# Strided sparse attention and a Mish MLP: strided v of every batch cast in flight, local q and k of batch 3 issued earlier, MLP1 opening with two strided halves

## The chip, the cores and the metric

The kernel runs on one core of a Trainium2 chip. The time is device microseconds of one execution; three runs of the kernel before gave 307.52, 309.35 and 312.32, median 309.35. The profile is of one further execution, in which every instruction and every DMA packet was recorded.

## The reference

There are 8 batches of 8 heads, 576 positions, head size 64, all in f32. Scores are `q k^T / 8`; heads 0 to 3 see the last 32 positions (local), heads 4 to 7 see positions congruent modulo 32 (strided). Softmax, times v. The result, seen as 4608 tokens of width 512, goes through an MLP with an activation:

```python
mask_local = (rel >= 0) & (rel < stride)                        # stride = 32
mask_strided = (rel >= 0) & (pos[None, :] % stride == pos[:, None] % stride)
attn = softmax(where(mask, scores, -1e9));  x = attn @ v        # 4608 x 512
h = x @ w_in                                                    # 512 x 2048
g = h * np.tanh(np.log1p(np.exp(h)))                            # Mish
out = g @ w_out                                                 # 2048 x 512
```

## The kernel before

**Blocks and batches.** The MLP works on nine blocks of 512 tokens, the attention on eight batches of 576. Both are interleaved on TensorE in an order written out by hand: block t consists of MLP1 (x times `w_in`, Mish on ScalarE into `gT`) and MLP2 (`gT` times `w_out`), and the attention of batch t+1 is threaded between the steps of MLP2 of block t, by the list `at`: at[i] runs after step i. Attention leaves its result transposed in `xT`, a ring of four batches: chunks 2 and 3 of `xT` are the strided heads, chunks 0 and 1 the local ones. Each product in `mlp1` adds the strided chunks (2, 3) first and the local ones (0, 1) after; group g covers two slices of 128 hidden columns in one accumulator of two PSUM banks, `accs[g % 3]` for g not of the form 3n+2, and single banks otherwise. For blocks 1 to 8 group 0 is split in its strided half and its local half, which run one after the other; the other seven groups follow whole.

MLP2 of block 0 is a plain product; its 16 steps end with two stores of 512 KB. MLP2 of blocks 1 to 7 uses seven products instead of eight (`mlp2_seven`): VectorE forms sums of `gT` and of `w_out`, and the results are copied and added up in two output tiles `osb`. The tiles come from a pool of three buffers. The first copy that ScalarE makes in block t is c22, into the second `osb` of the block; c11, VectorE's, goes into the first.

**Where q, k and v come from.** A batch's strided q and k are loaded on GpSimd's DMA queue, which converts f32 to bf16 on the way (`load_qk_str`, L119). Local q and k and local v are loaded as f32 on SP's queue (`load_qk_loc`, L133; `load_v_loc`, L169) and then cast by GpSimd (`cast_qk_loc`, `cast_v_loc`, L191). There is one f32 buffer for each: `kl32`, `ql32`, `vl32`. Strided v has two ways: for batches 0 to 2 it is loaded in bf16 on GpSimd's queue (`load_early_v_str`, L152) into one half of the buffer `vs32`, and spread from there into `vs` (`spread_v_str`); for batches 3 to 7 it is loaded as f32 on SP's queue (`load_v_str`, L143), into all of `vs32`, and cast by GpSimd (`cast_v`). Then SP transposes strided and local k and q of a batch by DMA (`transpose_by_dma`, L209 and L215), six instructions per batch from batch 2 on.

**The order on SP's queue.** SP issues in program order, and its instruction ends when its transfer has been passed on; the transfers of one queue run behind one another. In block 0, `load_rest2` runs after step 12 of MLP2: the six transposes of batch 2, then local v of batch 2. Then come block 0's two stores (after steps 13 and 15, L595), then, at the end of the block, local k and q, strided v and local v of batch 3. In a later block t: the transposes of batch t+2 (after step 10), the two stores of the block (L554), then the four loads of batch t+3.

**The order on GpSimd.** In block 0: casts of local v of batch 1 and of local k and q of batch 2; strided k and q of batch 3 (DMA); casts of local v of batch 2, which wait for its load. In block t from 1 to 4: strided k and q of batch t+3 (DMA, at the end of MLP1); the masks of the local scores of batch t+1 (L330); after step 9 of MLP2 the casts of batch t+2: local k, local q, strided v, local v.

In blocks 3 to 6 the last of the local attention (`late`) runs in the MLP1 of the next block, after its first, second and sixth entries.

Of the kernel before, what the change touches and what calls it, by code (L numbers as in the profile page):

```python
# [10 lines left out]
F32 = mybir.dt.float32  # L11
BF16 = mybir.dt.bfloat16
# [8 lines left out]
CS, PN = 8, 72  # L21
# [22 lines left out]
def kernel(ctx, tc, q, k, v, moe_w_in, moe_w_out, out):  # L44
    nc = tc.nc
    B, H, S, D = q.shape
# [9 lines left out]
    const = ctx.enter_context(tc.tile_pool(name="const", bufs=1))  # L56
# [8 lines left out]
    stm_bias = consts[0:PN, 128 + 2 * WQ + PN:128 + 2 * WQ + 2 * PN]  # L65
    zeros = const.tile([128, 512], BF16, name="zeros")
    vl32 = const.tile([128, 4, NW, D], F32, name="vl32")
    vs32 = const.tile([128, 4, CS, D], F32, name="vs32")
    ql32 = const.tile([128, 4, CL, D], F32, name="ql32")
    kl32 = const.tile([128, 4, CL, D], F32, name="kl32")  # L70
    ql = [const.tile([128, CL, 4, D], BF16, name=f"ql{i}") for i in range(2)]
# [4 lines left out]
    vs = [const.tile([128, 4, CS, D + 1], BF16, name=f"vs{i}") for i in range(2)]  # L76
# [23 lines left out]
    def acc(i, name):  # L100

        pool = ps_z[0] if i == 2 else ps_a
        return pool.tile([128, 2, 512], F32, tag=f"acc{i}", name=name)

    def bank(i, name):

        return ps_z[0].tile([128, 512], F32, tag=f"bank{i}", name=name)

    def split_third():

        third.close()
        ps_z[0] = third.enter_context(tc.tile_pool(name="psy", bufs=1, space=PS))
# [5 lines left out]
    def load_str(b, dst, src, h0=0):  # L118
        nc.gpsimd.dma_start(  # L119
            dst[b % 2][0:PN, h0:4, :], src[b, 4 + h0:8].rearrange("h (p j) d -> p h (j d)", j=CS)  # L120
        )

    def load_qk_str(b):
        load_str(b, ks, k)
        load_str(b, qs, q)
# [5 lines left out]
    def load_qk_loc(b):  # L131
        for dst, src in ((kl32, k), (ql32, q)):
            nc.sync.dma_start(  # L133
                dst[0:PL].rearrange("p h i d -> p (h i) d"),
                src[b, 0:4].rearrange("h (i p) d -> p (h i) d", p=PL),
            )
# [2 lines left out]
        for dst, src in ((kl, k), (ql, q)):  # L139
            nc.gpsimd.dma_start(by_head(dst[b]), src[b, 0:4].rearrange("h (p j) d -> p h (j d)", j=CL))  # L140

    def load_v_str(b):
        nc.sync.dma_start(vs32[0:PN], v[b, 4:8].rearrange("h (p j) d -> p h j d", j=CS))  # L143

    def vs_raw(b):

        flat = vs32[:].rearrange("p h j d -> p (h j d)").bitcast(BF16)
        b = b % 2
        return flat[0:PN, 2048 * b:2048 * b + 2048].rearrange("p (h x) -> p h x", h=4)

    def load_early_v_str(b):
        nc.gpsimd.dma_start(vs_raw(b), v[b, 4:8].rearrange("h (p j) d -> p h (j d)", j=CS))  # L152

    def spread_v_str(b, eng):
        cast(eng, vs[b % 2][0:PN, :, :, 0:D], vs_raw(b).rearrange("p h (j d) -> p h j d", d=D))

    def load_v_loc(b):

        w0 = 0
        if b == 0:
            w0 = 1
            nc.sync.dma_start(vl32[32:128, 0, 0, :], v[0, 0, 0:96, :])
        first = v[b, 0:1, 0:1, :].offset + (w0 * WQ - 32) * D
        src = bass.AP(v.tensor, first, [[D, 128], [WQ * D, 4 * NW - w0], [1, D]])
        nc.sync.dma_start(vl32[:].rearrange("p h w d -> p (h w) d")[:, w0:, :], src)  # L169

    def load_v(b):
        load_v_str(b)
        load_v_loc(b)

    def load_w_in(f0, f1):
        nc.gpsimd.dma_start(
# [10 lines left out]
    def cast(eng, out_, in_):  # L187
        if eng is nc.scalar:
            nc.scalar.copy(out_, in_)  # L189
        else:  # L190
            eng.tensor_copy(out_, in_)  # L191
# [15 lines left out]
    def transpose_by_dma(b):  # L207
# [5 lines left out]
        for hp in range(2):  # L213
            for src, dst in ((kl, kTl[:, hp, 32:32 + S]), (ql, qTl[:, hp, :])):
# [1 line left out]
                    dst.rearrange("c (i n) -> c i n", i=NW),  # L216
                    by_tile(src[b % 2])[:, hp].rearrange("p i e d -> p (i e d)"),
                )

    def cast_v(b, e_s, e_l):  # L220
        cast(e_s, vs[b % 2][0:PN, :, :, 0:D], vs32[0:PN])
        cast_v_loc(b, e_l)

    def cast_v_loc(b, eng, i0=0, i1=NW):
        for i in range(i0, i1, 3):
            cast(
                eng, vl[b % 2][:, i:i + 3, :, 0:D],
                vl32[:, :, i:i + 3, :].rearrange("p h w d -> p w h d"),
            )
        if i0 == 0:  # L230
            eng.memset(vl[b % 2][0:32, 0, :, 0:D], 0.0)
# [234 lines left out]
    def mlp1(t, accs):  # L466
        gT = g_pool.tile([128, 16, 512], BF16, tag="gT", name="gT")
        Sg = g_pool.tile([128, 4, 8, 256], BF16, tag="Sg", name="Sg") if t > 0 else None

        held, tiles = {}, {}  # L470

        def group(g, ccs=(2, 3, 0, 1)):
            single = t > 0 and g % 3 == 2
            if g not in held:
                if single:
                    held[g] = [bank(u, "psb") for u in range(2)]
                else:
                    ps = acc(accs[g % 3], "psh")
                    held[g] = [ps[:, u, :] for u in range(2)]
                    tiles[g] = ps  # L480
            for u in range(2):
                ps_u = held[g][u]
                fc = g + 8 * u if t > 0 else 2 * g + u
                for a, n, o in segs(t):
                    for cc in ccs:
                        nc.tensor.matmul(  # L486
                            ps_u[:, o:o + n], lhsT=w_in[:, cc, fc * 128:(fc + 1) * 128],
                            rhs=xT[:, cc, a:a + n], start=(cc == 2 and (o == 0 or len(ccs) == 4)),
                            stop=(cc == 1), skip_group_check=(len(ccs) < 4),
                        )  # L490
                if ccs[-1] == 1 and single:
                    nc.scalar.activation(gT[:, g + 8 * u, :], ps_u[:], AF.Mish)  # L492
            if ccs[-1] == 1:
                if not single:
                    to = gT[:, g::8, :] if t > 0 else gT[:, 2 * g:2 * g + 2, :]
                    nc.scalar.activation(to, tiles[g][:], AF.Mish)  # L496
                if t < B - 1 and g == 7:
                    nc.scalar.preload_act_table(AF.Exp)
                if t > 0 and g in SUMS_AT:
                    sums_g(gT, Sg, *SUMS_AT[g])  # L500
        if t == 0:
            halves = [[lambda g=g, c=c: group(g, c) for g in range(3)] for c in ((2, 3), (0, 1))]
            return gT, halves[0], halves[1] + [lambda g=g: group(g) for g in range(3, 8)]
        return gT, Sg, [lambda: (group(0, (2, 3)), group(0, (0, 1)))] + [
            lambda g=g: group(g) for g in range(1, 8)
        ]

    SUMS_AT = {3: (0, 4), 5: (4, 6), 6: (6, 7), 7: (7, 8)}

# [153 lines left out]
    with tc.manual_schedule():  # L663
        Po, Dv, Sc = nc.gpsimd, nc.vector, nc.scalar
# [6 lines left out]
        first = v[0, 0:1, 0:1, :].offset + 64 * D  # L671
# [21 lines left out]
        for h in (2, 3):  # L693
            first = v[0, h:h + 1, 0:1, :].offset - 32 * D
# [51 lines left out]
        gT, g1s, g1 = mlp1(0, accs)  # L746
# [22 lines left out]
        def load_rest2():  # L769
            transpose_by_dma(2)  # L770
            load_v_loc(2)
            load_qk_str(3)
            cast_v_loc(2, Po)

        for t in range(NBLK):
            if t == 0:
                x, y, z = accs
                (at, ts), late = attn_steps(1, y, y), {}
                at[0].append(cast_v1)
                at[12].append(load_rest2)  # L780
                at[15].append(lambda: spread_v_str(2, Dv))
                out_accs = (z, x)
            else:
                if t == 1:
                    split_third()
                x, y = 0, 1
                gT, Sg, g1 = mlp1(t, (x, y))
                now = late
                at, late = attn_steps(t + 1, x, y) if t + 1 < B else ([], {})
                if t + 2 < B:  # L790
                    at[10].append(lambda: transpose_by_dma(t + 2))
            for i, g in enumerate(g1):
                g()
                if t == 0:
                    for s in ts if i == len(g1) - 1 else ():
                        s()
                    continue
                if t == 1 and i == 0:
                    sums_w()
                for s in now.get(i, ()):  # L800
                    s()
            if 0 < t < B - 3:
                load_qk_str(t + 3)
            if t == 0:
                steps = mlp2(t, gT, out_accs, fc_major=True)
            elif t == NBLK - 1:
                mlp2_last(t, gT, Sg)
                break
            else:
                za, zc = [bank(i, "pso")[:].rearrange("p (n o) -> p n o", n=2) for i in range(2)]  # L810
                steps = mlp2_seven(t, gT, Sg, za, zc)
            for i, g in enumerate(steps):
                g()
                if i < len(at):
                    for s in at[i]:
                        s()
                if t > 0 and i == 9 and t + 2 < B:
                    cast_qk_loc(t + 2, Po, Po)
                    cast_v(t + 2, Po, Po)
            if t + 3 < B:  # L820
                load_qk_loc(t + 3)
                load_v(t + 3)


# [28 lines left out]
```

## Time and profile before

| what | value |
|---|---|
| runs | 307.52, 309.35, 312.32 us (median 309.35) |
| the profiled execution: its own time, its span | 308.23 us, 306.5 us |
| TensorE busy | 294.7 us (96%), 2900 matmuls and transposes |
| ScalarE, VectorE, GpSimd busy | 172.2, 152.4, 103.8 us |
| SP's DMA queue (q1) | 88120 packets, 33.00 MB, 62.6% of 16 engines |
| GpSimd's DMA queue (q0) | 14800 packets, 11.04 MB, 25.2% of 16 engines |
| stores of `osb` in the chain that ended last | 6% of the span |
| granted TensorE clock | 1.00 |

The span runs from the first to the last instruction. A busy share of TensorE near 100% does not say that nothing waits: matmul ends are modelled and pipelined. A row of a timeline gives start, duration, engine, line, operation and tiles, and in brackets the idle time in front of it with what ended it. An engine name with a q (SPq) is the engine's queue of instructions, here its DMA issues. Tiles are written output<-input, with buffer numbers left out. The chain is the sequence of work followed back from the last instruction; its rows give start, length and what.

### The profile page before, as it was taken

How to read it: one execution, taken by the hardware profiler on the slowest of the kernel's cores; microseconds unless marked ns; L12 is line 12 of the kernel's file. 1: busy time of each engine (PE TensorE's matmuls, PEld its weight loads, DVE VectorE, ACT ScalarE, POOL GpSimd, SP SyncE). 2: the span in 40 equal slices, each digit the busy share in tenths (PEclk: the TensorE clock that was granted, in tenths of full speed). 3: DMA queues.
4: the chain of work that ended last, by engine and by line, in shares of the span. 5: the costliest groups of instructions: out<-in, count | busy, mean ns of one | idle time of the engine just before them, and what ended most of it. 6: DMA issues, size and time to landing. Idle time of an engine off the chain costs nothing.

```text
span 306.5 us, 6863 instructions
## 1 busy us (share of the span) xinstructions
PE 294.7 (96%) x2900; PEld 198.5 (65%) x2922; DVE 152.4 (50%) x356; ACT 172.2 (56%) x220; POOL 103.8 (34%) x111
## 2 busy tenths in 40 slices
PE   8989999899999989999999999999999999999995
PEld 3554556445884568547888886468646874685484
DVE  2270165867670856256634753475437553720642
ACT  1568634667555665657556854676467646514530
POOL 8284502460664408620690059004900320000000
PEclk9999999999999999999999999999999999999999
DMA  8999999979999999999999999799950021003003
GB/s 155 185 203 186 194 195 193 168 123 157 263 141 182 156 250 186 163 134 260 182 169 116 262 188 156 189 180 187 131 161 0 3 98 41 2 0 139 0 0 139
DMA packets 103238, 44.72 MB, mean 146 GB/s; under 512 B 85672, under 2 KB 97272, under 8 KB 103208
## 3 DMA queue, kind: packets, MB, share of 16 engines
q1 hardware_dynamic: 88120, 33.00, 62.6%
q0 software_dynamic: 14800, 11.04, 25.2%
q8 instruction: 23, 0.38, 0.6%
q10 hardware_dynamic: 288, 0.25, 0.3%
q14 instruction: 7, 0.06, 0.1%
HBM read 38.38 MB, written 9.44 MB: 156 GB/s over the span
## 4 chain that ended last, share of the span: by engine, by line
PE 81%; DMA 9%; ACT 5%; DVE 3%; issue 2%; POOL 0%; ACTq 0%; POOLq 0%
PE psh L486 29%; PE pso L559 24%; PE psb L486 8%; DMA out_dram<-osb 6%; PE pso L587 4%; PE pso L614 4%; PE po L346 4%; PE ps L316 3%; DMA qs<-in_q_dram 3%; DVE x_l L372 2%; ACT Ps L324 1%; PE trx L395 1%; PE trx L385 1%; DVE osb L538 1%; ACT Pl L324 1%
## 5 line engine op out<-in xcount | busy, mean ns | idle before, releaser
L486 PE MATMUL psh<-xT,w_in 128*128 128x512 bf16 (+1 forms) x484 | 101.1, 358 | 1.7 <-ACT xT L189 0.8
L486 PEld LDWEIGHTS <-w_in 128*128 128x128 bf16 x640 | 61.4, 98 | 59.6 <-issue 2.3
L496 ACT ACTIVATE gT<-psh 128x1024 bf16<-128x1024 f32 x56 | 57.0, 1024 | 45.5 <-PE psh L486 45.5
L330 POOL TENSOR_TENSOR Pl<-Pl,consts_sb 128x960 bf16<-128x960 bf16 (+1 forms) x18 | 29.2, 1634 | 82.9 <-ACT Pl L324 82.4
L511 DVE TENSOR_TENSOR Sg<-gT 128x256 bf16<-128x256 bf16 (+2 forms) x64 | 27.2, 427 | 55.6 <-ACT gT L496 53.6
L559 PEld LDWEIGHTS <-Sg 128*128 128x128 bf16 x448 | 41.9, 98 | 6.2
L559 PE MATMUL pso<-Tw,Sg 128*128 128x256 bf16 x336 | 40.1, 273 | 0.0
L559 PEld LDWEIGHTS <-gT 128*128 128x128 bf16 x336 | 31.4, 98 | 4.6
L189 ACT COPY xT<-trx 128x576 bf16<-128x576 bf16 x32 | 20.1, 640 | 19.9 <-PE trx L395 13.9
L189 ACT COPY osb<-pso 128x512 f32<-128x512 f32 (+1 forms) x26 | 14.2, 545 | 29.3 <-PE pso L559 14.5
L486 PE MATMUL psb<-xT,w_in 128*128 128x512 bf16 (+1 forms) x141 | 30.1, 355 | 0.2
L559 PE MATMUL pso<-w_out,gT 128*128 128x256 bf16 x224 | 27.8, 273 | 0.0
L324 ACT ACTIVATE Pl<-ps 128x960 bf16<-128x960 f32 (+1 forms) x24 | 19.2, 808 | 11.7 <-PE ps L316 11.4
L538 DVE TENSOR_TENSOR osb<-pso,osb 128x512 f32<-128x512 f32 x21 | 14.5, 692 | 21.7 <-PE pso L559 20.0
L191 POOL CAST vl<-vl 128x768 bf16<-128x768 f32 x15 | 12.8, 881 | 27.2 <-DMA vl<-in_v_dram 27.2
L324 ACT ACTIVATE Ps<-ps 72x864 bf16<-72x864 f32 (+1 forms) x24 | 18.5, 804 | 4.9 <-PE ps L316 4.8
L492 ACT ACTIVATE gT<-psb 128x512 bf16<-128x512 f32 x32 | 19.0, 596 | 3.5 <-PE psb L486 3.5
L372 DVE TENSOR_TENSOR x_s<-po,rden 72x512 bf16<-72x512 f32 x28 | 19.2, 686 | 1.0
L330 DVE TENSOR_TENSOR Ps<-Ps,consts_sb 72x864 bf16<-72x864 bf16 (+1 forms) x21 | 12.2, 580 | 9.4 <-ACT Ps L324 8.8
L587 PE MATMUL pso<-w_out,gT 128*128 128x512 bf16 x59 | 15.8, 380 | 0.5 <-issue 0.3
L346 PEld LDWEIGHTS <-Ps 72*128 72x128 bf16 x256 | 12.1, 97 | 5.4 <-DVE Ps L330 1.7
L357 DVE RECIPROCAL rden<-po 96x4 f32<-96x4 f32 (+1 forms) x22 | 3.9, 177 | 22.1 <-PE po L346 22.0
(90 smaller groups left out, 346.3 us busy)
## 6 DMA issues: line engine op xcount, KB each, us to landing
out_dram<-osb SPq DMA_DIRECT2D x16, 512.0 KB, 4.8
vl<-in_v_dram SPq DMA_DIRECT2D x7, 768.0 KB, 11.2
kl<-in_k_dram SPq DMA_DIRECT2D x6, 576.0 KB, 10.2
ql<-in_q_dram SPq DMA_DIRECT2D x6, 576.0 KB, 13.1
vs<-in_v_dram SPq DMA_DIRECT2D x5, 576.0 KB
qs<-in_q_dram POOLq DMA_DIRECT2D x8, 288.0 KB, 8.9
w_in<-in_moe_w_in_dram POOLq DMA_DIRECT2D x4, 512.0 KB, 10.2
w_out<-in_moe_w_out_dram POOLq DMA_DIRECT2D x4, 512.0 KB, 17.2
```

The costliest lines, as they stand in the source:

```text
L189: nc.scalar.copy(out_, in_)
L324: nc.scalar.activation(pt[0:n, :, 0:nw], ps[0:n, :, o0:o0 + nw], AF.Exp, scale=scale)
L330: meng.tensor_tensor(out=pm, in0=pm, in1=mk[0:n, :].unsqueeze(1).unsqueeze(1).to_broadcast([n, 2, nu, w]), op=ALU.mult,)
L346: nc.tensor.matmul(po[:, h, :], lhsT=pt[0:n, c0:c0 + 128], rhs=rhs, start=True, stop=True,)
L372: nc.vector.tensor_tensor(out=dst.rearrange("p e (h d) -> p e h d", h=4), in0=po[0:m, :, :, 0:D], in1=rden[0:m].unsqueeze(3).to_broadcast( ...
L486: nc.tensor.matmul(ps_u[:, o:o + n], lhsT=w_in[:, cc, fc * 128:(fc + 1) * 128], rhs=xT[:, cc, a:a + n], start=(cc == 2 and (o == 0 or len( ...
L492: nc.scalar.activation(gT[:, g + 8 * u, :], ps_u[:], AF.Mish)
L496: nc.scalar.activation(to, tiles[g][:], AF.Mish)
L511: nc.vector.tensor_tensor(out=out_, in0=in0, in1=in1, op=op)
L538: add = lambda o, p: nc.vector.tensor_tensor(out=o, in0=p, in1=o, op=ALU.add)
L559: nc.tensor.matmul(ps[:, pair, :], lhsT=lhs(c, 128 * pair), rhs=rhs(c), start=(first and pair == 0 and c == 0), stop=(last and c == 7), sk ...
L587: nc.tensor.matmul(p[:, ot % 2, :], lhsT=gT[:, fc, 128 * ot:128 * ot + 128], rhs=w_out[:, fc, :], start=(fc == 0), stop=(fc == 15),)
```

## The change

Three edits. (1) Strided v of batches 3 to 7 is loaded as batches 0 to 2 were, in bf16 on GpSimd's queue, right behind strided k and q of the batch; the buffer is now a bf16 tile with two halves, `vsr`, of the same size as `vs32`; GpSimd spreads it into `vs` where it cast it before. SP no longer carries it. (2) The loads of local k and q of batch 3 move on SP's queue from behind block 0's two stores to a place in front of them, at the end of `load_rest2`'s SP work. (3) In the MLP1 of blocks 1 to 8 the strided half of group 1 runs between the two halves of group 0, and group 1's local half is the second entry of the list; the list keeps its eight entries.

```diff
-    vs32 = const.tile([128, 4, CS, D], F32, name="vs32")
+    vsr = const.tile([128, 2, 4, CS * D], BF16, name="vsr")
...
     def vs_raw(b):
-        flat = vs32[:].rearrange("p h j d -> p (h j d)").bitcast(BF16)
-        b = b % 2
-        return flat[0:PN, 2048 * b:2048 * b + 2048].rearrange("p (h x) -> p h x", h=4)
+        return vsr[0:PN, b % 2]
...
-        return gT, Sg, [lambda: (group(0, (2, 3)), group(0, (0, 1)))] + [
-            lambda g=g: group(g) for g in range(1, 8)
-        ]
+        first = [lambda: [group(*x) for x in ((0, (2, 3)), (1, (2, 3)), (0, (0, 1)))], lambda: group(1, (0, 1))]
+        return gT, Sg, first + [lambda g=g: group(g) for g in range(2, 8)]
...
         def load_rest2():
             transpose_by_dma(2)
             load_v_loc(2)
+            load_qk_loc(3)
             load_qk_str(3)
+            load_early_v_str(3)
             cast_v_loc(2, Po)
...
             if 0 < t < B - 3:
                 load_qk_str(t + 3)
+                load_early_v_str(t + 3)
...
                     cast_qk_loc(t + 2, Po, Po)
-                    cast_v(t + 2, Po, Po)
+                    spread_v_str(t + 2, Po)
+                    cast_v_loc(t + 2, Po)
             if t + 3 < B:
-                load_qk_loc(t + 3)
-                load_v(t + 3)
+                if t > 0:
+                    load_qk_loc(t + 3)
+                load_v_loc(t + 3)
```

More of the change, by code (lines that the diff above doesn't have):

```diff
@@ L140, in load_early_loc @@
             nc.gpsimd.dma_start(by_head(dst[b]), src[b, 0:4].rearrange("h (p j) d -> p h (j d)", j=CL))
-    def load_v_str(b):
-        nc.sync.dma_start(vs32[0:PN], v[b, 4:8].rearrange("h (p j) d -> p h j d", j=CS))
     def vs_raw(b):
-        flat = vs32[:].rearrange("p h j d -> p (h j d)").bitcast(BF16)
-        b = b % 2
-        return flat[0:PN, 2048 * b:2048 * b + 2048].rearrange("p (h x) -> p h x", h=4)
+        return vsr[0:PN, b % 2]
     def load_early_v_str(b):
@@ L169, in load_v_loc @@
         nc.sync.dma_start(vl32[:].rearrange("p h w d -> p (h w) d")[:, w0:, :], src)
-    def load_v(b):
-        load_v_str(b)
-        load_v_loc(b)
     def load_w_in(f0, f1):
@@ L218, in transpose_by_dma @@
                 )
-    def cast_v(b, e_s, e_l):
-        cast(e_s, vs[b % 2][0:PN, :, :, 0:D], vs32[0:PN])
-        cast_v_loc(b, e_l)
     def cast_v_loc(b, eng, i0=0, i1=NW):
```

## The prediction

> **What bounds the kernel now.** I read the span by stages first (windows cut where TensorE passes from MLP1 to MLP2), then ScalarE's order of time, the chain, and the queues behind it. Columns of the windows: stretch, its length, busy us of TensorE, its weight loads, VectorE, ScalarE, GpSimd (with counts), granted clock, DMA share, GB/s.
>
> ```profile
> 73.81:91.64 17.83, 17.35 (x253) 15.14 (x252) 12.32 (x28) 11.15 (x15) 9.97 (x10) 1.00 1.25 202
> 105.71:124.77 19.06, 17.54 (x254) 15.18 (x253) 11.78 (x28) 11.15 (x15) 8.24 (x8) 1.00 1.22 212
> 138.84:155.99 17.15, 16.89 (x240) 14.48 (x239) 10.96 (x26) 11.31 (x14) 8.10 (x8) 1.00 1.24 218
> ```
>
> These are the MLP2 stages of blocks 1, 2 and 3. TensorE bounds the kernel (294.7 us busy of 306.5); block 3 shows the clean stage, 17.15 us. Block 1 loses 0.7 us and block 2 loses 1.9 us. What they wait for is in ScalarE's timeline (brackets: idle time before, and what ended it):
>
> ```profile
> 79.77 0.59 ACT L189 COPY osb<-pso 128x512 f32<-128x512 f32 x1 [1.75 <-DMA out_dram<-osb]
> 112.89 0.59 ACT L189 COPY osb<-pso 128x512 f32<-128x512 f32 x1 [2.98 <-DMA out_dram<-osb]
> ```
>
> and in the chain (start, length, what):
>
> ```profile
> 67.36 12.33 DMA out_dram<-osb
> ...
> 106.84 5.94 DMA out_dram<-osb
> ```
>
> The output tiles `osb` rotate through three buffers. Block 1's second tile is the third one taken after block 0's first, so its first ScalarE copy (c22) may start only when block 0's **first store** has landed, at 67.36 + 12.33 = 79.7. ScalarE runs in order and the next exponentials stand behind that copy; TensorE needs them for the local scores. So this landing has no slack at all: it holds ScalarE 1.75 us already. Block 2 hangs on block 1's first store in the same way.
>
> The store's data was ready at 57.2. It is late because of SP's queue (start, duration of the issue):
>
> ```profile
> 65.41 1.23 SPq L215 DMA_TRANSPOSE qTl<-ql  x1
> 66.69 0.58 SPq L169 DMA_DIRECT2D vl<-in_v_dram  x1
> 67.36 8.37 SPq L595 DMA_DIRECT2D out_dram<-osb  x2
> 75.78 0.88 SPq L133 DMA_DIRECT2D kl<-in_k_dram  x1
> 76.71 4.95 SPq L133 DMA_DIRECT2D ql<-in_q_dram  x1
> 81.77 8.34 SPq L143 DMA_DIRECT2D vs<-in_v_dram  x1
> 90.22 0.40 SPq L169 DMA_DIRECT2D vl<-in_v_dram  x1
> ```
>
> The reader sees an SP that is never idle here: an issue of 5 to 8 us is an issue held back by transfers not yet drained. Landings from the issue lists (issue plus time to landing) come in the order of issue: local v of batch 2 at 66.69 + 11.2 = 77.9, the stores at 79.7 and 81.8 (75.31 + 6.5), local k and q of batch 3 at 87.1 and 93.0.
>
> **The edit ahead of the stores.** The new `load_qk_loc(3)` in `load_rest2` puts these two loads, 576 KB each, between local v of batch 2 and block 0's first store on SP. Their buffers are free (GpSimd's casts of batch 2 end at 64.5), so nothing holds them but the queue. Their price, from the issue lists of 66 to 92 us, then of 108 to 126 us:
>
> ```profile
> kl<-in_k_dram SPq DMA_DIRECT2D x1, 576.0 KB, 11.3
> ql<-in_q_dram SPq DMA_DIRECT2D x1, 576.0 KB, 16.3
> ```
> ```profile
> kl<-in_k_dram SPq DMA_DIRECT2D x1, 576.0 KB, 9.7
> ql<-in_q_dram SPq DMA_DIRECT2D x1, 576.0 KB, 12.0
> ```
>
> In the second pair they follow a store landed at 114.2 and land at 117.7 and 120.9: 6.7 us for both, with no GpSimd load in flight. In the first pair they follow the store of 81.8 and take 11.2 us, beside two GpSimd loads (qs and ks of batch 4). So a GpSimd load beside them costs about (11.2 - 6.7)/2 = 2.2 us. The queues' lists for 74:76, where SP's queue is alone, and for 82:88, say the same (packets, MB, share of 16 engines):
>
> ```profile
> q1 hardware_dynamic: 1631, 0.42, 135.0%
> ```
> ```profile
> q0 software_dynamic: 772, 0.57, 83.4%
> q1 hardware_dynamic: 1230, 0.31, 52.6%
> ```
>
> SP's queue (q1) moves 815 packets a us alone and 205 beside GpSimd's (q0).
>
> Do GpSimd's loads of batch 4 fall into this stretch again? They stand behind the cast of batch 2's local v, which starts when that has landed:
>
> ```profile
> 77.93 1.97 POOL L191 CAST vl<-vl 128x768 bf16<-128x768 f32 x2 [12.04 <-DMA vl<-in_v_dram]
> ...
> 80.09 0.72 POOL L119 DMA_DIRECT2D ks<-in_k_dram  x1
> ```
>
> They do. And the change makes them three, since strided v of batch 4 follows on the same queue; strided v of batch 3 likewise follows ks and qs of batch 3 at 65.9, ahead of local v of batch 2. The sum for the first store's landing: 79.7, plus 2.0 for v of batch 3 (0.834 x 6 us x 288/772 packets = 1.9; a load beside costs 2.2), plus 6.7 for k and q, plus 5.0 for the batch-4 loads (three at 2.2 make 6.6; I let the last fall partly behind the store) = 93.4. Bounds: 86.4 if no GpSimd load counts; 97 if all count and SP's queue runs empty for 2 us, as between 90 and 92, when it moved 465 packets instead of 1630. I take 93.4, nearest to the row of 11.2 us, the same two loads in the same place. The c22 copy, and all behind it on ScalarE, TensorE, VectorE and GpSimd's masks, comes **13.7 us** later than now (bounds 6.7 and 17.3).
>
> **What is given back.** Batch 3's k and q are there before block 1's casts, and strided v's issue leaves SP: the transposes of batch 3 and then block 1's stores no longer wait, relative to TensorE, as they do up to 106.84. Block 2's 1.9 us go. Nothing is late next: blocks 3 to 6 have clean MLP2 stages (17.15 to 17.2) in front of an SP that was later than it will be now. -1.9 (0 if the delayed stretch repeats the pattern).
>
> **MLP1's order.** Four matmuls of group 1 (0.216 us each, 1.73 per 8) move ahead of group 0's local half, which waits for the last copy of xT:
>
> ```profile
> 60.87 2.75 PE L486 MATMUL psh<-xT,w_in 128*128 128x512 bf16 x12 [0.81 <-ACT xT L189]
> ```
>
> At block 1 the cover is worth up to 0.8 us, but the landing time ends block 1's next stage whatever TensorE did before: nothing. At blocks 2 and 3 the four matmuls end 0.25 us before the copy does (91.64 + 0.86 against 92.76): -0.5 for both, 0 to -0.75. Blocks 4 to 8 show no such wait: 0. The first Mish comes 0.86 us later; ScalarE idles 1.17 us ahead of it, and that accumulator is wanted again only by group 3, 5.2 us in: 0, or 0.9 at most once if the cover is gone.
>
> **Strided v on GpSimd.** Its 288 packets leave q1 and join q0, about 1.9 us of the engines' time either way. Each load costs GpSimd 0.70 us of issue (as L152 does for batches 0 to 2), queued behind it are masks before which GpSimd idles 10 to 19 us (1.3 in block 1): 0. The cast then reads bf16 instead of f32, 72x2048 on GpSimd: that form is not in the trace; its f32 twin takes 1.89, and anything between 0.7 (VectorE's copy of this form) and 3 disappears in the same idle time. The local transposes wait for the k and q casts ahead of it, not for it. 0.
>
> **TensorE's clock.** While ScalarE is held, TensorE stops at the local scores (now 0.44 us before 81.32), then for some 14 us. What a rest does shows only at the start:
>
> ```profile
> 1.20 6.43 PE L270 MATMUL un<-zeros 128*128 128x512 bf16 x16 [1.20 <-DVE zeros L678]
> ```
>
> 402 ns each against 216 later: 3.0 us lost on sixteen. Rests of under 1 us cost nothing. So 0 to +3.0; a rest of 14 us is nearer to the start, and as some matmuls behind it wait for exponentials anyway I take +2.0. The Trainium skill (TensorE: Matmul & The Clock Gate, Part 1: The HAM clock gate) says that about 3.4 us without work halve the clock and that about 3.4 us of work restore it, an estimated 1.7 us here instead of 2.0; the profile's granted clock, 1.00 throughout, begins its records too late to show the start, so no row decides.
>
> **Sum.** 13.7 - 1.9 - 0.5 + 2.0 = +13.3 on the profiled execution's 308.23 (span 306.5): 321.5. That execution lies 1.1 under the median of the runs, 309.35; I say **322**. From the median, 2% (303.2 to 315.5) is about what a measurement of this kernel can tell from no change.
>
> **Rivals.** (1) The same wait, short: no GpSimd load counts and the clock holds: 6.7 - 1.9 - 0.5 = +4.3, 312.5 to 314. For it: q0's share is an average, and the loads could land after the store. Against: the 11.2 us row. 0.17. (2) Not slower: the store does not queue behind the loads. It has 512 packets of 2 KB with its twin against the loads' 4608, and if SP's issues spread over engines that drain unevenly, it lands near 79.7; then only the gains are left: -1.9, -0.5 and up to 1.5 of block 1: 304.5 to 306. The point is a landing by 80. The skill (DMA: Bandwidth & Descriptors, Queues, rings and completion order) says that completion is not first-in-first-out per issuing engine; by that alone it would be 305.5. Every landing that the issue lists give for SP's loads and stores stands in order. 0.10. (3) No late store, but three GpSimd loads hold the next transposes: 2.2 us a block in blocks 2 to 4 less the slack of some 5 us: about 310 to 313. 0.05. The forecast: 0.68.
>
> The range 312 to 328 takes in rival 1, the bounds of the landing (97 gives 325) and of the clock, with 1 for the median; it leaves out rival 2 and part of 3. Faster by over 2% needs 6 us, more than all gains: 0.03. Within 2%: rivals 1 to 3 less that, 0.29. Slower: the forecast's 0.68.
>
> **What would show it.** ScalarE's first `osb` copy of block 1 waits over 10 us for a store; kl and ql of batch 3 issue on SP ahead of it; block 2's copy has no such wait; MLP2 of block 1 lasts some 30 us; the granted clock dips behind it. I am wrong if that copy starts by 82.

## The result, and the profile after

The change makes the kernel slower: median 320.58 us of four runs (320.35 to 322.52), against 309.11 of four runs of the kernel before (307.52 to 312.32). The ratio is 1.0403, 95% interval 1.0339 to 1.0467. The prediction was 322, with a range of 312 to 328. The profiled execution took 320.55 us, span 318.8, so it is compared with the 308.23 and 306.5 of before: 12.3 us more. Executions more than 1.5% above the fastest of their kernel are left out of the ratios, not of the medians.

The windows of MLP2 in blocks 1, 2 and 3 of the changed kernel (columns as in the prediction):

```profile
72.36:105.79 33.43, 19.06 (x253) 16.04 (x252) 11.75 (x28) 11.15 (x15) 12.31 (x14) 0.80 1.05 172
119.61:137.02 17.41, 17.28 (x253) 14.99 (x252) 11.87 (x28) 11.37 (x15) 8.35 (x8) 1.00 0.99 147
150.84:167.99 17.15, 16.88 (x239) 14.48 (x238) 10.98 (x26) 11.31 (x14) 8.10 (x8) 1.00 1.06 161
```

Block 1 takes 33.4 us instead of 17.8, at a granted clock of 0.80; block 2 falls from 19.1 to 17.4; block 3 is unchanged. ScalarE's timeline has the c22 copy of block 1, and the chain the store in front of it:

```profile
92.20 0.59 ACT L180 COPY osb<-pso 128x512 f32<-128x512 f32 x1 [15.64 <-DMA out_dram<-osb]
```
```profile
67.97 7.99 SPq L133
76.01 4.12 SPq L133
80.23 11.89 DMA out_dram<-osb
```

The chain that before went from the store's issue at 67.36 to its landing at 79.7 now runs through the issues of local k and q (L133), and the store lands at 80.23 + 11.89 = 92.1. The 15.64 us of idle time in front of the copy were 1.75. GpSimd's timeline shows the three loads of batch 4 in the same stretch, behind the cast of batch 2's local v, as costed:

```profile
78.88 1.60 POOL L182 CAST vl<-vl 128x768 bf16<-128x768 f32 x2 [12.82 <-DMA vl<-in_v_dram]
...
80.67 0.72 POOL L119 DMA_DIRECT2D ks<-in_k_dram  x1
81.38 0.71 POOL L119 DMA_DIRECT2D qs<-in_q_dram  x1
82.08 0.71 POOL L147 DMA_DIRECT2D vsr<-in_v_dram  x1
...
105.28 1.89 POOL L182 COPY vs<-vsr 72x2048 bf16<-72x2048 bf16 x1
```

The last row is the spread of strided v, 1.89 us, as long as the f32 cast that it replaces. TensorE's timeline and the clock row of the page (tenths in 40 slices of 8.0 us) show the rest and what follows it:

```profile
93.76 0.58 PE L303 MATMUL ps<-qTl,kTl 64*128 64x96 bf16 x10 [14.33 <-ACT Pl L311]
94.28 3.44 PE L545 MATMUL pso<-w_out,Sg 128*128 128x256 bf16 x16
...
98.21 1.92 PE L545 MATMUL pso<-Tw,Sg 128*128 128x256 bf16 x16
```
```profile
PEclk9999999999758999999999999999999999999999
```

After 14.33 us without work, sixteen matmuls take 3.44 us; the next sixteen take 1.92 again. The low digits of the clock row cover 80 to 104 us: the clock falls during the rest and is back soon behind it.

### The profile page after: what moved, and what is told of

Its sections match the earlier page's. It is cut to its first block, busy times and chain, and to the rows that moved or that the text cites. A ratio compares the mean times of both kernels' runs of the same rounds, so it can differ in the third digit from the quotient of the medians.

```text
span 318.8 us, 6857 instructions
## 1 busy us (share of the span) xinstructions
PE 295.1 (93%) x2900; PEld 199.0 (62%) x2922; DVE 151.4 (48%) x356; ACT 171.7 (54%) x220; POOL 106.2 (33%) x116
## 3 DMA queue, kind: packets, MB, share of 16 engines
q1 hardware_dynamic: 86620, 30.05, 53.3%
q0 software_dynamic: 16800, 12.51, 26.5%
## 4 chain that ended last, share of the span: by engine, by line
PE 81%; DMA 6%; SPq 4%; DVE 3%; ACT 2%; issue 1%; POOL 0%; ACTq 0%; POOLq 0%
PE psh L473 28%; PE pso L545 25%; PE psb L473 8%; PE pso L573 4%; PE po L333 4%; PE pso L600 4%; SPq L133 4%; DMA out_dram<-osb 4%; PE ps L303 3%; DMA qs<-in_q_dram 3%; DVE x_l L359 2%; PE trx L372 1%; ACT Ps L311 1%; PE trx L382 1%; DVE osb L524 1%
## 5 line engine op out<-in xcount | busy, mean ns | idle before, releaser
L483 ACT ACTIVATE gT<-psh 128x1024 bf16<-128x1024 f32 x56 | 56.3, 1024 | 45.2 <-PE psh L473 45.1
L545 PEld LDWEIGHTS <-Sg 128*128 128x128 bf16 x448 | 42.6, 100 | 7.0
L311 ACT ACTIVATE Pl<-ps 128x960 bf16<-128x960 f32 (+1 forms) x24 | 19.2, 808 | 13.3 <-PE ps L303 13.1
L303 PE MATMUL ps<-qTl,kTl 64*128 64x96 bf16 x192 | 8.2, 208 | 14.4 <-ACT Pl L311 14.3
L182 POOL CAST vl<-vl 128x768 bf16<-128x768 f32 x15 | 12.0, 827 | 25.5 <-DMA vl<-in_v_dram 25.5
L573 PE MATMUL pso<-w_out,gT 128*128 128x512 bf16 x59 | 15.8, 380 | 0.5 <-issue 0.3
## 6 DMA issues: line engine op xcount, KB each, us to landing
vsr<-in_v_dram POOLq DMA_DIRECT2D x8, 288.0 KB, 12.4
```

The lines of the kernel that those rows point to most:

```text
L303: nc.tensor.matmul(ps[:, e, o:o + w], lhsT=lhsT, rhs=rhs, start=not biased, stop=True, skip_group_check=biased,)
L311: nc.scalar.activation(pt[0:n, :, 0:nw], ps[0:n, :, o0:o0 + nw], AF.Exp, scale=scale)
L545: nc.tensor.matmul(ps[:, pair, :], lhsT=lhs(c, 128 * pair), rhs=rhs(c), start=(first and pair == 0 and c == 0), stop=(last and c == 7), sk ...
L573: nc.tensor.matmul(p[:, ot % 2, :], lhsT=gT[:, fc, 128 * ot:128 * ot + 128], rhs=w_out[:, fc, :], start=(fc == 0), stop=(fc == 15),)
```

## The experiments

One table first: from the first matmul of one stage to the first of the next, in the profile of each run (us), with the ratio to the kernel before. The kernel before was timed anew beside each group of runs, with medians of 307.29, 308.12 and 308.74. What the names stand for is told run by run below.

| run | MLP1 of block 1 | MLP2 of block 1 | MLP1 of block 2 | MLP2 of block 2 | ratio, 95% interval |
|---|---|---|---|---|---|
| before | 14.78 | 17.83 | 14.07 | 19.06 | 1 |
| after | 13.94 | 33.43 | 13.81 | 17.41 | 1.0403 (1.0339 to 1.0467) |
| k and q alone | 14.78 | 31.69 | 14.07 | 17.42 | 1.0382 (1.0317 to 1.0448) |
| v alone | 14.78 | 23.67 | 14.07 | 18.19 | 1.0130 (1.0073 to 1.0186) |
| MLP1 order alone | 13.94 | 17.88 | 13.81 | 22.16 | 1.0004 (0.9964 to 1.0043) |
| v and MLP1 order (k, q back) | 13.94 | 22.81 | 13.81 | 18.82 | 1.0157 (1.0098 to 1.0216) |
| after, c22 kept elsewhere | 13.94 | 22.27 | 13.82 | 20.24 | 1.0206 (1.0131 to 1.0281) |
| after, block 0's stores first | 13.94 | 23.17 | 13.81 | 17.48 | 1.0089 (1.0055 to 1.0123) |
| after, GpSimd's loads later | 13.94 | 30.45 | 13.81 | 17.42 | 1.0341 (1.0276 to 1.0406) |
| after, 56 matmuls in the wait | 13.94 | 33.94 | 13.81 | 17.41 | 1.0421 (1.0352 to 1.0491) |
| after, 64 matmuls in the wait | 13.94 | 32.91 | 13.81 | 17.41 | 1.0372 (1.0313 to 1.0431) |
| before, MLP1 order, loads later | 13.94 | 17.81 | 13.81 | 17.42 | 0.9883 (0.9800 to 0.9966) |
| the same, and c22 kept elsewhere | 13.94 | 17.32 | 13.81 | 17.41 | 0.9887 (0.9840 to 0.9933) |

Behind block 2 all stages agree within 0.55 us between these profiles; ahead of block 1 the MLP2 of block 0 takes 17.9 to 18.8. What the edits cost shows in the MLP2 of blocks 1 and 2.

### The three edits, one by one

**k and q alone**, on the kernel before:

```diff
             load_v_loc(2)
+            load_qk_loc(3)
             load_qk_str(3)
...
-                load_qk_loc(t + 3)
+                if t > 0:
+                    load_qk_loc(t + 3)
```

> The kernel before with this one edit: local k and q of batch 3 ahead of block 0's stores. Theory: the store lands at 79.7 plus 6.7 to 11.2 us (two GpSimd loads beside it instead of three), 86.4 to 91; with block 2's wait gone and 1.5 to 2 us of slow clock the time is 313 to 320 us. Rival (the loads alone cost little, it takes three GpSimd loads beside them): under 312 us.

Measured: 319.73 us, ratio 1.0382, at the upper end of the theory's span. ScalarE's timeline:

```profile
91.35 0.58 ACT L189 COPY osb<-pso 128x512 f32<-128x512 f32 x1 [13.37 <-DMA out_dram<-osb]
```

The store lands at 91.3. This one edit makes nearly all of the loss; the rival falls.

**k and q put back**, the other two edits kept (the two lines above undone in the changed kernel):

> The changed kernel with local k and q of batch 3 put back behind block 0's two stores; strided v on GpSimd's queue and the new order of MLP1 stay. Theory (the two loads ahead of the store are the loss): the first store lands near 81, one us later than in the kernel before for strided v of batch 3 beside it, ScalarE's c22 copy of block 1 waits some 3 us, time 306.5 to 310 us. Rival (strided v on GpSimd's queue is the loss): the wait of over 10 us stays and the time is over 315 us.

Measured: 312.36 us against 307.29, ratio 1.0157. The loss falls by more than half, so the two loads carry most of it, but the time lies above the theory's 310. c22 waits 5.06 us for a store that lands at 81.6, and block 2's copy waits 2.74 us again. So the other two edits are not free; the next two runs take them one by one.

**Strided v alone**, and **the order of MLP1 alone**, on the kernel before (the hunks of the change as they are):

> The kernel before with strided v of batches 3 to 7 cast in flight on GpSimd's queue alone. Reading from the run with k and q put back: the three GpSimd loads squeeze SP's queue ahead of both late stores, so block 1's store lands 1 to 2 us later and block 2's 2 to 3 us later than in the kernel before; time 2 to 4 us over it. Rival (the packets only change queue, as the prediction had it): within 1 us of it.

> The kernel before with the new order of MLP1 alone. Theory: MLP1 of blocks 1, 2 and 3 each save a wait, 0.8, 0.25 and 0.25 us, but block 1 still ends its wait with the landing of block 0's first store; time 0.3 to 1.0 us under the kernel before. Rival (the later first Mish or the later local attention costs): 0.5 us or more over it.

Strided v alone: 311.52 us against 308.12, ratio 1.0130; the reading has the time right and both landings a little early, and the prediction's equal exchange of queues does not hold. ScalarE's timeline, then TensorE's:

```profile
82.26 0.58 ACT L180 COPY osb<-pso 128x512 f32<-128x512 f32 x1 [4.95 <-DMA out_dram<-osb]
```
```profile
83.82 0.59 PE L303 MATMUL ps<-qTl,kTl 64*128 64x96 bf16 x10 [3.64 <-ACT Pl L311]
84.33 3.59 PE L546 MATMUL pso<-w_out,Sg 128*128 128x256 bf16 x16
```

On SP's queue strided v came behind the stores; on GpSimd's it runs beside the transposes and stores that the next stage waits for. Block 0's first store lands at 82.2 instead of 79.7 and block 1's at 117.1 instead of 112.8. The loss is that of the whole change on a smaller scale: of the 5.8 us that block 1's MLP2 takes longer, 3.2 lie in front of the c22 copy and 2.7 behind it, where sixteen matmuls take 3.59 us instead of 1.92 after a rest of 3.64 us.

That strided v delays SP's queue is seen in more than one pair of profiles: local v of batch 2 lands at 75.6 to 77.9 in five profiles without strided v beside it and at 78.8 to 82.3 in eight with it and the same order on SP's queue up to there. These widths also say how far one profile can differ from the next.

The order of MLP1 alone: 308.09 against 308.12, no difference, where 0.3 to 1.0 us of gain was expected. Its MLP1 stages are shorter as costed (14.78 to 13.94, 14.07 to 13.81), and in the profiled execution (309.42 us, near the slowest of twelve, 305.70 to 309.63) the time comes back in block 2 as a longer wait for batch 3's transposes, from TensorE's timeline:

```profile
112.05 0.22 PE L316 MATMUL ps<-qTl,kTl 64*128 64x96 bf16 x2 [2.98 <-DMA qTl<-ql]
```

### Is it the wait for the store, or the traffic?

The first try gave block 0's first output another buffer:

```diff
+                if ot == 1:
+                    held_o = xT[:, :, 3 * S:3 * S + 512].bitcast(F32)
+                    nc.scalar.copy(held_o, p[:].rearrange("p o (h d) -> p (o h) d", h=2))
+                    for o in range(2):
+                        nc.sync.dma_start(out[...], held_o[:, 2 * o:2 * o + 2, :])
+                    return
```

> The changed kernel, but block 0's first output goes from a free part of xT instead of an osb buffer, in two stores of 256 KB; so no copy of block 1 has to wait for it, while all transfers keep their order. Theory (the wait for that store's landing is all there is to it): the store still lands near 92, but ScalarE's c22 copy starts at once, TensorE's clock stays full, time 304 to 308 us. Rival (the traffic itself holds TensorE, by late transposes or loads): 314 us or more, with a wait on another transfer in the place of the store's.

Measured: 338.72 us, ratio 1.1013, far from both. Now it is ScalarE's next write into `xT`, to other columns, that waits for the store, from 59 us on:

```profile
92.64 1.18 ACT L180 COPY xT<-trx 128x576 bf16<-128x576 bf16 x2 [33.51 <-DMA out_dram<-xT]
```

The run does not tell wait from traffic, but it shows one thing cleanly: TensorE stood still for 33 us and the store still landed at 92.5. Its landing does not depend on how far TensorE has come.

The second try moves the early write instead. In block 1, c22 stays in the `zeros` tile until the block's end:

```diff
+        c22_end = c22
+        if t == 1:
+            c22 = zeros[:].rearrange("p (n o) -> p n o", n=2)
...
         def store(h):
+            if h == 1 and c22_end is not c22:
+                nc.vector.tensor_copy(c22_end, c22)
```

> The changed kernel, but in block 1 the partial sum c22 is kept in bf16 in the zeros tile (free after the start) and copied into its osb buffer at the end of the block, so no early copy of block 1 writes the buffer of block 0's first store; all transfers keep their order. (The tile xT, tried for this before, made its own next writer wait.) Two extra roundings to bf16 and one VectorE copy. Theory (that one wait is all): the store still lands near 92, TensorE's wait of 14.3 us and the slow clock go, at most 2 us wait is left at the end of block 1 and 1 to 3 us in block 2, time 305 to 310 us. Rival (traffic or late transposes hold TensorE anyway): over 314 us.

Measured: 314.02 us against 308.12, ratio 1.0206, at the rival's edge. The theory's 310 is missed. The 14.3 us wait and the slow clock behind it are gone, with the store landing at 94.2. In their place TensorE waits for GpSimd's masks in block 1 and for batch 3's transposes in block 2:

```profile
88.17 0.43 PE L333 MATMUL po<-vl,Pl 128*128 128x65 bf16 x8 [2.72 <-POOL Pl L317]
...
115.39 0.22 PE L303 MATMUL ps<-qTl,kTl 64*128 64x96 bf16 x2 [1.96 <-DMA qTl<-ql]
```

and block 2's copy waits 4.16 us for block 1's first store. The masks stand behind three GpSimd loads, and these behind the cast of batch 2's local v:

```profile
82.12 1.60 POOL L182 CAST vl<-vl 128x768 bf16<-128x768 f32 x2 [14.43 <-DMA vl<-in_v_dram]
...
86.11 4.83 POOL L317 TENSOR_TENSOR Pl<-Pl,consts_sb 128x960 bf16<-128x960 bf16 x3
```

So about half of the loss goes with the wait for the store (1.0403 to 1.0206), and late masks and transposes are the next to be late once it is gone. A slow clock is left as well: from 90.3 to 93.0 us it is granted at 0.50, and eight matmuls take 1.90 us instead of 1.04. The run with v alone shows neither of the two waits on TensorE; what it loses is the store's wait and the clock.

**Block 0's stores first**: the changed kernel with the order strided transposes, the two stores, local transposes, local v of batch 2, local k and q of batch 3.

```diff
-                at[12].append(load_rest2)
+                at[12].append(lambda: transpose_str(2))
+                at[15].append(load_rest2)
```

> The changed kernel with block 0's two stores moved ahead of batch 2's local transposes and of everything behind these on SP's queue (strided transposes, stores, local transposes, local v of batch 2, local k and q of batch 3). The local transposes wait for GpSimd's casts until 61 to 64 anyway, and the stores are ready at 57 and 60. Theory: the first store lands by 72, no copy waits in blocks 1 and 2, the gains of the change stand alone: 303 to 306 us. Rival (the local transposes of batch 2, or GpSimd's loads behind them, come too late for block 1): 308 us or more, with a wait on them at 78 to 84.

Measured: 310.46 us against 307.29, ratio 1.0089 (1.0055 to 1.0123): the rival. The first store lands at 64.4 and no copy of block 1 waits, but local v of batch 2, now behind two stores and beside three GpSimd loads, lands at 83.0 instead of 78.8 in the changed kernel. GpSimd's cast, loads and masks follow it:

```profile
89.07 0.43 PE L333 MATMUL po<-vl,Pl 128*128 128x65 bf16 x8 [3.72 <-POOL Pl L317]
```

Behind this rest the granted clock is 0.55 from 91.0 to 93.5 us.

### The terms of the sum

**GpSimd's loads of batch 4 after the stretch**:

```diff
-            if 0 < t < B - 3:
+            if 1 < t < B - 3:
                 load_qk_str(t + 3)
...
+                if t == 1 and i == 9:
+                    load_qk_str(4)
+                    load_early_v_str(4)
```

> The changed kernel, but GpSimd's three loads of batch 4 are issued after step 9 of block 1's MLP2, behind the masks, and no longer while k and q of batch 3 and block 0's first store are under way. Theory (these loads delay SP's queue by 4 to 6 us there): the store lands at 86.5 to 88.5 instead of 92.1 and the time falls by 3 to 5 us against the changed kernel, to 315.5 to 317.5, less what the moved loads cost in block 2. Rival (SP's queue is slow by itself, by its own back-pressure): the store lands after 91 and the time stays.

Measured: 318.21 us against 308.74, ratio 1.0341; its profiled span is 315.9 against 318.8. The store lands at 88.4:

```profile
88.47 0.59 ACT L180 COPY osb<-pso 128x512 f32<-128x512 f32 x1 [11.86 <-DMA out_dram<-osb]
```

Against the changed kernel's profile the three loads cost the store 92.1 - 88.4 = 3.7 us. The rest of the delay, 8.7 us, is k and q themselves and strided v of batch 3. The theory has the landing right, but the time falls by less than its 3 to 5 us: by the ratios (1.0403 to 1.0341) by some 2 us, and their intervals overlap.

How sure is the 3.7? In three other profiles with the same order on the queues (c22 kept elsewhere, 56 and 64 matmuls) the store lands at 93.3 to 94.2. Much of that comes from an earlier point, the landing of local v. Counted from there, the store lands 9.3 us later in this run, 13.3 in the changed kernel and 11.2 to 12.7 in those three: 1.9 to 4.0 us for the loads. With k and q alone, beside only two GpSimd loads, it is 13.7. So a third load adds nothing that can be seen; in the changed kernel the three land at 88.2, 91.4 and 95.0, the last behind the store.

**TensorE kept busy**: `unread(56)`, then `unread(64)`, behind step 4 of block 1's MLP2 in the changed kernel. `unread(n)` issues n matmuls of zeros whose result nothing reads.

> The changed kernel with 56 matmuls of zeros (12.1 us of TensorE at full clock) put into TensorE's wait in block 1, behind step 4 of its MLP2; they change no result. Theory (the rest slows the clock, which costs 1.5 to 2 us behind it): the clock stays at 1.00 and the time is 1 to 2 us under the changed kernel, 318.5 to 319.7 us. Rival (the slow clock is a symptom without a price, matmuls there waiting anyway): within 0.5 us of the changed kernel.

> As the run with 56 matmuls of zeros in TensorE's wait of block 1, now with 64 (13.8 us), since a rest of 3.1 us was left there, behind which 16 matmuls took 3.08 us instead of 1.92. Theory: with a rest of under 2 us the clock holds, the stage from ScalarE's c22 copy to block 2's MLP1 takes 11.9 us as in the kernel before (13.6 in the changed one, 13.2 with 56). Rival (the stage is longer for another reason): it stays at 13 us or more with 16 matmuls in 1.92.

With 56: 320.84 us, ratio 1.0421 (1.0352 to 1.0491), no gain to be seen; 3.11 us of rest remained, and the clock still fell (granted 0.60 from 94.9 to 98.6 us; with 64 it is 1.00 there). With 64: 319.34 us, ratio 1.0372. TensorE's timelines of the two:

```profile
94.94 0.58 PE L303 MATMUL ps<-qTl,kTl 64*128 64x96 bf16 x10 [3.11 <-ACT Pl L311]
95.45 3.08 PE L545 MATMUL pso<-w_out,Sg 128*128 128x256 bf16 x16
```
```profile
95.12 0.39 PE L303 MATMUL ps<-qTl,kTl 64*128 64x96 bf16 x10 [1.57 <-ACT Pl L311]
95.44 1.92 PE L545 MATMUL pso<-w_out,Sg 128*128 128x256 bf16 x16
```

The whole times overlap, so the stage decides: from the start of the c22 copy to block 2's MLP1 it is 11.87 us before (79.77 to 91.64), 13.59 after (92.20 to 105.79), 13.22 with 56 and 11.89 with 64. The slow clock costs 1.7 us, and filling the rest gives them back.

### A version faster than both

The runs say what to keep off the path: no load ahead of block 0's stores, and no GpSimd load beside the transposes and stores that block 2 waits for. So the kernel before, with the new order of MLP1, and strided k and q of batches 5 to 7 loaded after step 9 of MLP2; in the second run also c22 of blocks 1 and 2 in `zeros`:

```diff
-            if 0 < t < B - 3:
+            if t == 1:
                 load_qk_str(t + 3)
...
+                if 1 < t < B - 3 and i == 9:
+                    load_qk_str(t + 3)
```

> The kernel before with the new order of MLP1 and GpSimd's loads of batches 5 to 7 after step 9 of MLP2, without the bf16 copy. Theory: the transposes of batch 3 and block 1's first store, with no GpSimd load beside them, land 3 to 4 us earlier, block 2's wait goes and block 1's stays: 1 to 2.5 us under the kernel before. Rival (the traffic only moves on and holds block 3): within 0.5 us of it or slower.

> The kernel before with the new order of MLP1, c22 of blocks 1 and 2 kept in bf16 in the zeros tile until the end of the block (so neither block waits for an early store), and GpSimd's loads of batches 5 to 7 issued after step 9 of MLP2 instead of at the end of MLP1, so that they do not run beside the transposes and stores that the next stage waits for. No transfer is moved ahead of block 0's stores. Theory: block 1's and block 2's waits (0.7 and 1.9 us) and MLP1's (1.3 us) go, 1.5 to 4 us under the kernel before. Rival (batch 3's transposes, limited by the traffic before them, become the next wait): within 1 us of it.

Measured: 306.86 us (304.34 to 310.22) and 304.44 us (303.90 to 305.73) against 308.74; ratios 0.9883 (0.9800 to 0.9966) and 0.9887 (0.9840 to 0.9933). Block 2's MLP2 takes 17.4 us in both instead of 19.1. The run with the order of MLP1 alone differs from the first of the two only in the place of GpSimd's loads, and there block 2's MLP2 took 22.16. With the copy held back block 1's falls from 17.8 to 17.3 as well, but in the time this can't be told apart. The order of MLP1, worth nothing alone, shortens the stages of MLP1 by 1.4 us here as it did there; no run takes it out of this version, so what it is worth in the whole time is not shown.

## Why the prediction was right, point by point

**What bounds the kernel, and the edit ahead of the stores.** Right, in mechanism and place: one landing without slack, delayed by two loads that were put in front of it on a queue whose loads and stores land, in every profile here, in the order of issue. The terms of the landing:

| term | predicted | measured | from |
|---|---|---|---|
| strided v of batch 3 beside local v of batch 2 | 2.0 | 1.0 | local v lands at 78.8 (77.9) |
| local k and q of batch 3 | 6.7 | 7.5 | the store 9.3 us behind local v with no GpSimd load beside (1.8 before) |
| three GpSimd loads of batch 4 | 5.0 | 4.0 | the store 13.3 us behind local v against 9.3 |
| landing of the first store | 93.4 | 92.1 | 79.7 + 1.0 + 7.5 + 4.0, less 0.1 of rounding |

The sizes are known to two microseconds or so, no better: they come from single profiles, and with the same order on the queues the store lands at 92.1 to 94.2. The forecast of 93.4 lies among these, so its 1.3 us are no error that these runs can show, and that the whole came within 1.5 us of 322 is in part luck. Strided v is the least sure: the middle of local v's landings is 80.1 with it and 76.5 without, 3.6 us and not 1.0. The price of 2.2 us for a GpSimd load beside SP's queue stands: two loads cost 13.7 - 9.3 = 4.4 us in the run of k and q alone, and in the changed kernel, where two of the three land ahead of the store, they cost 4.0. One reading was wrong on the way: strided v is 400 packets on GpSimd's queue and 300 on SP's (for five loads GpSimd's queue goes from 14800 to 16800 packets and SP's from 88120 to 86620), not 288 on both, so the same working would have given 2.6 us instead of 1.9.

**What is given back.** Right in size: 19.06 to 17.41, -1.65 against -1.9, and nothing late behind it. The reason given, early k and q and strided v off SP's queue, is not what the runs show: with c22 kept elsewhere both are the same, and block 2's MLP2 takes 20.24 us. In the table of stages block 2 goes by how late block 1 ends, whichever edits are in: where block 1's MLP2 takes 17.8 or 17.9 and GpSimd's loads are not moved, block 2's takes 19.06 and 22.16, at 22.3 to 23.7 it takes 17.48 to 20.24, and from 30 on 17.4. A late block 1 gives SP's queue time to get ahead. One thing that it moves is GpSimd's loads of batch 5, here before and after:

```profile
102.01 0.78 POOL L119 DMA_DIRECT2D ks<-in_k_dram  x1
105.31 0.70 POOL L119 DMA_DIRECT2D qs<-in_q_dram  x1 [2.52 <-DMA qTs<-qs]
```
```profile
108.91 0.78 POOL L119 DMA_DIRECT2D ks<-in_k_dram  x1
109.68 0.71 POOL L119 DMA_DIRECT2D qs<-in_q_dram  x1
```

Before, they run beside batch 3's transposes and block 1's first store, issued up to 105.49 and at 106.84. In the changed kernel GpSimd is held up by the late stage too, and they follow both, issued up to 107.18 and at 108.50. Moved behind step 9 in the faster version, with k and q where they were before, they leave the same 17.42. So the 1.65 us came with the delay itself; that the forecast had them nearly right is luck.

**MLP1's order.** -0.26 and -0.25 at blocks 2 and 3 (14.07 to 13.81 and 13.82), as costed, and nothing at block 1, since the landing ends the next stage. Alone, the edit gains nothing either (1.0004): in its profile a wait in block 2 takes the gain.

**Strided v on GpSimd.** This step failed as it was put: "0", its packets only changing queue. The casts' part was right (1.89 us for 1.89). But moved to GpSimd's queue, the load also moves in order, from behind the stores to beside them, and alone this costs 1.3%, by a later store and the slow clock behind it. The sum held all the same because it charged strided v a second time, inside the landing. Beside the other edits no cost of it can be told from the noise (1.0403 against 1.0382 for k and q alone); that block 1's long wait covers it is likely, but no run shows it.

**TensorE's clock.** +1.7 against +2.0. The trace's own start bounded it by 3.0; the Trainium skill's rule (TensorE: Matmul & The Clock Gate, Part 1: The HAM clock gate), by which the estimate was 1.7, agrees with the measured 13.59 - 11.87 = 1.72. Its 3.4 us without work are more than this case needed: a rest of 3.11 us slowed the clock.

**The sum.** 12.4 (79.77 to 92.20) - 1.65 - 0.5 + 1.7 = 12.0, and 0.3 in the last stage (15.5 to 15.8), for which no run gives a cause: 12.3. Predicted 13.3: the landing came 1.3 us and the clock 0.3 under the forecast, and 0.25 less was given back.

**The rivals.** The short wait: its price for k and q was nearly right (6.7 against 7.5), but GpSimd's loads count and the clock does not hold. The store that does not queue behind the loads: it lands behind them in every run that has them ahead, at 88.4 to 94.2. A page of the skill spoke for that rival (DMA: Bandwidth & Descriptors, Queues, rings and completion order: completion is not first-in-first-out per issuing engine); no run here shows it for SP's loads and stores. Late transposes through GpSimd's loads: not in the changed kernel, but it is what the run with c22 kept elsewhere finds underneath.

## What to carry to other kernels

Before a load is moved up a queue, look for what then stands behind it: here 1.1 MB put ahead of a 512 KB store held a buffer that the next block needed, and 12 us of DMA queue became 12 us of kernel. A load that changes its queue also changes its place in the order, and beside a late transfer it can cost something even when the same data is loaded. A wait that ends a stage hides the next ones, so a saving in front of it (MLP1's order) is worth nothing until that wait is gone.

## What was not expected

- A part of a tile is not always a buffer of its own: with the store reading one batch's columns of `xT`, ScalarE's writes to other columns waited 33.5 us for it. Each of the two stores read a strided slice over two chunks; whether its being strided is the cause was not tried.
- A rest of 3.1 us was enough to slow TensorE: sixteen matmuls in 3.08 us instead of 1.92. After 1.57 us they took 1.92. Between the two there is no sharp line to be read: with c22 kept elsewhere eight matmuls behind a rest of 2.72 us took 1.04 us as usual, and eight from 90.92 on took 1.90.
- Moving three pairs of GpSimd loads from the end of MLP1 to after step 9 of MLP2 made the kernel 1.2% faster (0.9883, 0.9800 to 0.9966, together with an order of MLP1 that alone gave 1.0004), with not one byte less to move.
